# Fused attention, dense FFN and routed experts on one core: tiles moved back to multiples of 64 bytes, one block's routing put off, values one step later, two more staging tiles

## The chip, the cores and the metric

One core of one Trainium2 chip runs the whole program in one launch. The metric is the device time of one execution in microseconds (us); the kernel before was run three times, and the median is what the change is measured against. The profiled execution is a separate one, with its own time.

## The reference, cut to what matters

Three stages, one behind the other, in float32:

- attention over 8 batches, 8 heads, 576 tokens, with keys and values first averaged over groups of 8 tokens, so that each head has 72 keys;
- a dense feed-forward layer on the 4608 tokens of 512 numbers: `x @ w_in` (512 by 2048), ELU, `@ w_out` (2048 by 512);
- a routed layer: each token's row times `w_gate` gives 8 logits, the largest picks an expert, its softmax weight is the gate; the token goes through `relu(x @ w1[e]) @ w2[e]` of that expert (512 by 1024, 1024 by 512), and the result is scaled by the gate.

```
x = attention(q, pool8(k), pool8(v))
x = elu(x @ w_in) @ w_out
e = argmax(x @ w_gate);  out = gate_w * (relu(x @ w1[e]) @ w2[e])
```

## The kernel before, in words

**Precision.** Every large product is made of three float32r products: operands are split into a high part and a remainder (`xh`, `xl`; `gh`, `gl`; `wih`, `wil`; `woh`, `wol`; in the routed stage `zh`, `zl`, `m1h`, `m1l`, `hh`, `hl`, `m2h`, `m2l`), and high*high, high*low and low*high are added up in PSUM. TensorE is given a weight load and a matmul for each, 512 moving columns where a block has four tiles of 128 tokens, 384 where it has three.

**Blocks and steps.** The 36 token tiles are ten blocks: 0 to 3 of three tiles, 4 to 9 of four. A step is one of 16 slices of 128 hidden units of one block. `g1_mm` (L514) makes 12 matmuls into `h` (moving `xh`/`xl`, stationary `wih`/`wil`); `elu_a`, `elu_b`, `elu_c` (L527 to L546) run on ScalarE and VectorE and leave `gh` and `gl`; two steps later `g2` (L554) makes three matmuls a tile into `y` (stationary `gh`/`gl`, moving `woh`/`wol`). Blocks 0 and 1 take turns in quarters (steps 0 to 31, numbered by their place in `steps`); from step 32 each block has its 16 steps. Block 9's begin at step 144, and its end overlaps the routed stage.

**What rides along.** Beside the two products a step carries slices of other work, put into named slots by `at(n, slot, fn, ...)` (L727) and run by `step` (L893) in a fixed order: `pre`, the `h` matmuls, `pe_mid`, `dve_first`, `dve_pre`, ELU, `act_hi`, `act_mid`, the `y` matmuls, `pe_end`, `evac`, `dve_mid`, `elu_c`, `act_end`, `end`. Each engine takes its instructions strictly in that written order. For an attention tile `t` this is: `s_mm` (L409), scores, at `SCORE[t]`; `s_exp` and `s_norm` in that step and the next; `q_turn` (L455), a transpose on VectorE, one step on; `q_move` (L462) in two parts in the next two steps, whose 32-partition copies into `aT` are shared by ScalarE and VectorE; `pv_mm` (L485), the product with the values, at `VALUE[t]`; `pv_copy` (L496), which splits it into `xh` and `xl`. The last value tile must be through before a block's first step. `PLAN` (L757) gives the steps of a block's score products relative to the block before, and L769 the steps of the value products.

**Routing.** `route_at` (L862) spreads a block's logits over some ten steps. A logit of one tile and one expert is one VectorE instruction on 512 numbers (`r_logit` L619, into `junk`) against an expert's row that SyncE has loaded (`r_gate_load` L614, three buffers `wgb`). Then `r_top`, `r_weight` (which also makes SyncE store the rows with their gate to `ybuf`, L675), and, two steps after that, `r_count` (two small matmuls into `pos` on TensorE, L690) and `r_put` (L697), which lets GpSimd scatter the token numbers into `tab`. `pos` takes a PSUM bank from the ring of three that `sp` and `pv` use (`bank_a` L158; from step 62 a ring of two, `bank_z`). Block 0's logits (`route_at(0, 40, ...)`, L883) lie in steps 40 to 50, block 2's in 51 to 59, block 3's in 66 to 75, block 4's from step 82 on.

**The routed stage.** `mix(n)` (L1621) is a step of 24 + 24 matmuls (`mhD` L1358, `myD` L1395) on 512 tokens of one expert. `ahead(n)` (L1527) is the planner: by due times (`STEP`, reach 36 for loads, 25 for splits) it issues `m_load`, SyncE's loads of a quarter of an expert's two matrices into staging tiles, and `m_split`, the split on ScalarE and VectorE (L135, L136) into W slots. Staging tiles are numbered: 0 lies in the pool `p2a`, 2 to 4 in `p2b` (`free_s`, L1674); a D unit takes two, and gives them back at its split. By the planner's rules a load is written once a step, in the same step as the split whose tiles it takes over. `chores` (L1607) puts block 9's logits into steps 0 to 3 of this stage (eight a step), `r_top`, `r_weight`, `r_place`, `lists_rest` into steps 4 to 7.

**Where tiles lie.** On the left of each partition: `cpool`, then `wpool` (32 slots W of 4096 bytes, which hold `wih` to `wol` and later `m1h` to `m2l`), then `apool` and `spool`, whose place `p2a` takes in the routed stage. On the right, from the top down: `mrpool`, then `m1pool`, whose place `p2b` takes. Tiles are rounded up to 32 bytes. The starts in the program before, as the remainder by 512:

```
W slots 32 | hh, hl 32 | zh, zl 288      (routed stage: W, p2a)
gh, gl and xh, xl of blocks 0 3 5 7 9: 352   (m1pool)
xh, xl of blocks 1 2 4 6 8: 480              (apool)
```

All slices that matmuls take inside these tiles step by multiples of 512 bytes, so the remainder holds for each of them. All are 32 past a multiple of 64.

Of the kernel before, what the change touches and what calls it, by code (L numbers as in the profile page):

```python
# [10 lines left out]
F32 = mybir.dt.float32  # L11
# [8 lines left out]
P = 128  # L20
# [10 lines left out]
START = [sum(SIZES[:x]) for x in range(NBLK + 1)]  # L31
# [3 lines left out]
NF = DFF // P  # L35
NE = 8
KC = DM // P
ROW = DM + 1
# [64 lines left out]
def fused_kernel(ctx: ExitStack, tc: tile.TileContext, q, k, v, w_in, w_out, w_gate, w1, w2, cst, out):  # L103
# [3 lines left out]
    cpool = ctx.enter_context(tc.tile_pool(name="cpool", bufs=1))  # L107
# [12 lines left out]
    def const(at, n):  # L120
        return small[:, at - C_W:at - C_W + n]
# [4 lines left out]
    eidx, part = const(C_E, NE), const(C_J, 1)  # L126
# [14 lines left out]
    m1_ctx = ExitStack()  # L141
    at_ctx = ExitStack()
    mrpool = ctx.enter_context(tc.tile_pool(name="mrpool", bufs=1, side="right"))
    m1pool = m1_ctx.enter_context(tc.tile_pool(name="m1pool", bufs=1, side="right"))
    apool = at_ctx.enter_context(tc.tile_pool(name="apool", bufs=1))
    spool = at_ctx.enter_context(tc.tile_pool(name="spool", bufs=4))
# [26 lines left out]
    free_w, slot_w = list(range(W_SLOTS - 1)), {"sums": W_SLOTS - 1}  # L173

    def w_tile(shape, dtype, name):
        slot_w[name] = k = free_w.pop(0)
        return wpool.tile(shape, dtype, tag=f"W{k}", bufs=1, name=name)

    def w_free(*names):
        for name in names:  # L180
            free_w.append(slot_w.pop(name))
# [327 lines left out]
    ys, yrows, lgs, pes = {}, {}, {}, {}  # L509
# [64 lines left out]
    def y_rows(blk, plus=None):  # L574
        yr = mrpool.tile([P, TB, ROW], F32, tag="yr", name=f"yr{blk}")
        yrows[blk] = [yr[:, j] for j in range(TB)]
        if SIZES[blk] > TB:
            if blk < last - 1:
                yrows[blk].append(spool.tile([P, S], F32, tag="st", name=f"yx{blk}")[:, :ROW])
            else:  # L580
                yrows[blk].append(w_tile([P, ROW], F32, f"yx{blk}"))
        for j, r in enumerate(yrows[blk]):
            if plus:
                nc.vector.tensor_add(r[:, :DM], plus[j], ys[blk][j])
            elif j < 2:
                nc.scalar.copy(r[:, :DM], ys[blk][j])  # L586
            else:
                nc.vector.tensor_copy(r[:, :DM], ys[blk][j])
        return yr
# [68 lines left out]
    def r_weight(blk):  # L658
        lg = lgs.pop(blk)
        mx, mb, eq = tops.pop(blk)  # L660
        yr = yrows[blk]
        nb = SIZES[blk]
        pool = lpool["p"] if blk == NBLK - 1 else mrpool

        def small_tile(shape, tag, dtype=F32):
            return pool.tile(shape, dtype, tag=tag, name=f"{tag}{blk}")

        se = mrpool.tile([P, nb], F32, tag="rse", name=f"rse{blk}")
        nc.vector.tensor_reduce(se, lg, axis=AX.X, op=ALU.add)
        nc.vector.tensor_scalar_add(se, se, 1e-9)  # L670
        for j in range(nb):
            nc.vector.reciprocal(yr[j][:, DM:ROW], se[:, j:j + 1])
        for j in range(nb):
            r = P * (START[blk] + j)
            nc.sync.dma_start(ybuf[r:r + P, :], yr[j])  # L675
        if f"yx{blk}" in slot_w:
            w_free(f"yx{blk}")
        nc.vector.tensor_mul(eq, eq, wge.unsqueeze(1).to_broadcast([P, nb, NE]))
        nc.vector.tensor_reduce(mx, eq, axis=AX.X, op=ALU.max)
        oh = small_tile([P, nb, NE], "roh", BF16)  # L680
        nc.vector.tensor_tensor(oh, eq, mb, op=ALU.is_equal)
        for j in range(nb):
            nc.vector.tensor_add(acc[:, j + 1], acc[:, j], oh[:, j])
        routed[blk] = oh, [small_tile([P, nb, NE], "rpe"), small_tile([P, nb], "rpf"), small_tile([P, nb], "rpi", I32)]
# [38 lines left out]
    LAG = 2  # L723
    last = NBLK - 1
    events = {}

    def at(n, slot, fn, *args):  # L727
        events.setdefault((n, slot), []).append((fn, args))
# [12 lines left out]
    def turn_at(t, n):  # L741
        at(n + 1, "end", q_turn, t)
        for part in range(2):
            at(n + 2 + part, "act_end" if part and t == START[4] else "act_mid", q_move, t, part)

    def trans_at(t, n):
        at(n, "pe_end" if t in OUT else "pe_mid", t_mm, t)
# [6 lines left out]
    at(2 * NF - 2, "end", s_wide)  # L754
    first_of = {b: b * S // P for b in range(B)}
    SCORE = {6: (20, "pe_mid"), 7: (24, "pe_mid"), 8: (28, "pe_mid")}
    PLAN = {3: (-1, 4, 9), 4: (-2, 2, 6, 10), 5: (-3, 1, 4, 8)}  # L757
    TRANS = {6: 23, 7: 26, 8: 30}
    OUT = {
        6: ((28, "pe_end"), (29, "pre")),  # L760
        7: ((29, "pe_end"), (30, "pre")),
        8: ((31, "pe_mid"), (31, "act_mid")),
    }
    VALUE = {}
    for t in range(START[3], NT):
        blk, j = BLOCK[t]
        SCORE[t] = (NF * (blk - 1) + PLAN.get(blk, (-4, 0, 4, 8))[j], "pe_mid")
        if t > START[3]:
            VALUE[t - 1] = SCORE[t][0] + (t == START[5]) + 2 * (t > START[5])  # L769
    VALUE[NT - 1] = NF * (NBLK - 1) - 2  # L770
    for t in range(2 * TB, NT):
        if t >= START[3]:
            if t > T_TURN:
                at(VALUE[t - 1], "pe_mid", pv_mm, t - 1)
                at(VALUE[t - 1], "act_mid", pv_copy, t - 1)
            at(SCORE[t][0] - 6, "end", a_load, t)
# [7 lines left out]
    at(NF * 4 - 2, "end", early.update, {"two": True})  # L784
    at(VALUE[NT - 1], "pe_mid", pv_mm, NT - 1)
    at(VALUE[NT - 1], "act_mid", pv_copy, NT - 1)
    for b in range(2, B):
        n0 = SCORE[first_of[b]][0]
# [44 lines left out]
    for x, (w, c) in enumerate(chunks):  # L833
        n = 2 + x
# [24 lines left out]
    for x in range(8):  # L859
        at(QF + 1 + x // 2, "end", gate_copy, x)  # L860

    def route_at(blk, n0, per):  # L862
        at(n0 - 3, "end", r_gate_load, blk, 0)
        at(n0 - 2, "end", r_gate_load, blk, 1)
        at(n0 - 1, "end", r_gate_load, blk, 2)
        n = 0
        nb = SIZES[blk]
        for x in range(NE * nb):
            e, j = divmod(x, nb)
            at(n0 + n, ("dve_mid", "end", "end", "end")[x - sum(per[:n])], r_logit, blk, e, j)  # L870
            if j == nb - 1 and e + 3 < NE:
                at(n0 + n, "end", r_gate_load, blk, e + 3)
            if x + 1 == sum(per[:n + 1]):
                n += 1
        n += n0
        at(n, "dve_mid", r_top, blk)
        at(n + 1, "dve_mid", r_weight, blk)
        if blk < last - 1:
            at(n + 3, "pe_mid", r_count, blk)
            at(n + 3, "end", r_put, blk)  # L880

    route_at(1, 30, [2, 3, 3, 1, 1, 2, 3, 3, 3, 3])
    route_at(0, 40, [2] * 9 + [3, 3])  # L883
    route_at(2, 3 * NF + LAG + 1, [2, 2, 3, 3, 3, 3, 2, 3, 3])
    for blk in range(3, last):
        per = [4, 3, 3, 3, 3, 3, 4, 3, 3, 3] if SIZES[blk] > TB else [3, 2, 3, 2, 3, 2, 3, 2, 2, 2]
        route_at(blk, NF * (blk + 1) + LAG, per)

    def run(n, slot):
        for fn, args in events.pop((n, slot), ()):  # L890
            fn(*args)
# [131 lines left out]
    def new(shape, name, dtype=F32):  # L1023
        return lpool["p"].tile(shape, dtype, name=name)
# [6 lines left out]
    def counts(tag):  # L1031
        pc = bank_z([P, NE], f"cp{tag}")
        nc.tensor.matmul(pc, ones, acc[:, 0], start=True, stop=True)
        cnt = new([P, NE], f"cnt{tag}")
        nc.vector.tensor_copy(cnt, pc)
        return cnt
# [99 lines left out]
    def lists_first():  # L1136
        full = above(counts("w"), thrf[:, 1::2], "w")
        regs, oh, _ = make_list(full, basee, KD, "w", 2 * ST)
        used = cpool.tile([P, NE], F32, name="used")
        nc.vector.tensor_add(used, oh[:, 0], oh[:, 1])  # L1140
        for s in range(2, KD):
            nc.vector.tensor_add(used, used, oh[:, s])
        nc.vector.tensor_scalar_mul(used, used, 2.0)
        for s in range(KD):
            where["D", s] = (regs, s)
        lpool["used"] = used
# [26 lines left out]
    pools = []  # L1173
# [3 lines left out]
    free_s, slot_s = [0], {}  # L1177
# [314 lines left out]
    n0 = len(steps) - NF  # L1492
# [67 lines left out]
    for k in range(1, len(main)):  # L1560
        kind, prev = main[k][0], main[k - 1][0]
        for u in range(TILES[kind]):
            if kind == "T":
                n = 4 * k - 2
            elif prev == "T":
                n = 4 * k - TILES[kind] + u
            else:
                n = 4 * k - 1
            (trans_late if prev != "T" and u > 1 else trans_at).setdefault(n, []).append((main[k], u))
    moves, casts_first = {}, set()  # L1570
    for k in range(TURN_FROM, len(main)):
        it, far = main[k], main[k - 1][0] == "T"
        if it[0] != "T":
# [3 lines left out]
            n = 4 * k - 4 if far else 4 * k - 1  # L1577
# [20 lines left out]

    def logits(n):
        nb = SIZES[last]  # L1600
        for x in range(2 * nb * n, 2 * nb * (n + 1)):
            e, j = divmod(x, nb)
            r_logit(last, e, j)
            if j == nb - 1 and e + 3 < NE:
                r_gate_load(last, e + 3)

    chores = {n: [(logits, n)] for n in range(4)}  # L1607
    chores[4] = [(r_top, last)]
    chores[5] = [(r_weight, last)]
    chores[6] = [(r_place, last)]  # L1610
    chores[7] = [(lists_rest,)]
    chores[8] = [(make_lists, 0)]
    chores[11] = [(make_lists, 1)]

    def index(x, *fns):
# [55 lines left out]
        y_evac(last)  # L1671
    m1_ctx.close()
    pools.append(ctx.enter_context(tc.tile_pool(name="p2b", bufs=1, side="right", reuse_waits="tile")))
    free_s += [2, 3, 4]  # L1674
    with tc.manual_schedule(engines=ENGINES):
        ahead(0)
        for n in range(7):
# [94 lines left out]
```

## Time and profile before

| | us |
|---|---|
| median of 3 runs | 1375.26 (1372.09 to 1376.05) |
| profiled execution, its own time | 1370.78 |
| its span, first to last instruction | 1369.0 |
| TensorE busy in the span | 1341.8 (98%) |
| VectorE busy | 1016.8 (74%) |
| ScalarE busy | 796.6 (58%) |

TensorE is busy nearly throughout, but "busy" counts an instruction from its start to its modelled end: how fast matmuls follow each other has to be read from the chain of waits, which gives stretches of matmuls with start, length and count. In the listings below PE is TensorE, DVE VectorE, ACT ScalarE, POOL GpSimd, SP SyncE (SPq its queue).

### The profile page before, as it was taken

The numbers are of one execution on the slowest core, as the hardware profiler recorded it, in microseconds if no ns is written. First come the engines' busy times: TensorE is split into PE (matmuls) and PEld (weight loads), VectorE is DVE, ScalarE is ACT, GpSimd is POOL, SyncE is SP. The second block draws the span as 40 slices with busy tenths as digits, with TensorE's granted clock in tenths as the row PEclk, the third lists the DMA queues.
The fourth block names the chain that finished last, engine by engine and source line by source line (L and its number), as shares of the span: only waits on it lengthen the run. The fifth ranks groups of instructions, "written<-read, shape, count | busy, mean of one in ns | idle before, by whom it ended". The sixth has DMA issues, their size and how long they took to land.

```text
span 1369.0 us, 22633 instructions
## 1 busy us (share of the span) xinstructions
PE 1341.8 (98%) x7977; PEld 1097.4 (80%) x7978; DVE 1016.8 (74%) x2301; ACT 796.6 (58%) x1855; POOL 276.5 (20%) x249
## 2 busy tenths in 40 slices
PE   8999999989999999999999999999999999999998
PEld 5798888878777777777777777888777888878787
DVE  7899889878787797796886886875867756747362
ACT  6777866757766656666666654462355445536261
POOL 4665411011112111121100000111213130222010
PEclk9999999989999999999999999999999999999999
DMA  9367535666657347349216202746686557597580
GB/s 337 123 188 211 148 82 111 56 104 46 96 64 92 38 78 76 30 81 88 37 35 70 32 24 39 125 121 93 185 138 117 168 173 234 197 304 243 196 281 23
DMA packets 107203, 167.26 MB, mean 122 GB/s; under 512 B 15501, under 2 KB 53007, under 8 KB 107024
## 3 DMA queue, kind: packets, MB, share of 16 engines
q1 hardware_dynamic: 89224, 131.25, 42.1%
q0 software_dynamic: 17856, 34.46, 12.8%
q8 instruction: 65, 1.06, 0.4%
q14 instruction: 58, 0.48, 0.2%
HBM read 144.26 MB, written 23.98 MB: 123 GB/s over the span
## 4 chain that ended last, share of the span: by engine, by line
PE 84%; DVE 5%; issue 4%; DMA 3%; ACT 3%; SPq 1%; POOL 1%; POOLq 0%; another core or an unknown queue 0%; ACTq 0%; DVEq 0%
PE y L564 28%; PE h L520 28%; PE mhD L1358 11%; PE myD L1395 11%; PE pv L492 3%; PE sp L423 2%; DMA w2stD<-in_moe_w_dram 1%; DVE junk L626 1%; DMA oidxT<-tab 1%; PE vsum L358 1%; POOL out_dram L1418 1%; DMA natv<-in_v_dram 0%; DVE g L537 0%; PE uh L1439 0%; DVE aT L467 0%
## 5 line engine op out<-in xcount | busy, mean ns | idle before, releaser
L564 PE MATMUL y<-woh,gh 128*128 128x512 f32 x576 | 234.1, 406 | 0.1
L564 PE MATMUL y<-wol,gh 128*128 128x512 f32 x576 | 228.1, 396 | 0.0
L564 PE MATMUL y<-woh,gl 128*128 128x512 f32 x576 | 228.1, 396 | 0.0
L530 ACT ACTIVATE th<-h 128x512 f32<-128x512 f32 (+1 forms) x160 | 89.0, 556 | 189.9 <-PE h L520 189.4
L537 DVE SCALAR_TENSOR_TENSOR g<-g,th 128x512 f32<-128x512 f32 (+1 forms) x160 | 102.6, 641 | 105.7 <-ACT th L532 104.9
L520 PE MATMUL h<-xh,wih 128*128 128x512 f32 (+1 forms) x640 | 162.1, 375 | 1.4 <-ACT xh L506 1.4
L520 PE MATMUL h<-xl,wih 128*128 128x512 f32 (+1 forms) x640 | 160.3, 372 | 0.1
L520 PE MATMUL h<-xh,wil 128*128 128x512 f32 (+1 forms) x640 | 159.4, 371 | 0.0
L626 DVE SCALAR_TENSOR_TENSOR junk<-yr,wgb 128x512 bf16<-128x512 f32 x216 | 148.5, 688 | 6.1 <-ACT yr L586 2.5
L1372 ACT ACTIVATE hhD<-mhD 128x512 fp32r<-128x512 f32 x64 | 38.3, 599 | 173.7 <-PE myD L1395 166.7
L544 ACT CAST gh<-g 128x512 fp32r<-128x512 f32 (+1 forms) x160 | 92.9, 580 | 78.5 <-DVE g L538 62.8
L520 PEld LDWEIGHTS h<-xh,wih 128*128 128x128 f32 x640 | 117.8, 189 | 24.3 <-ACT xh L506 1.9
L520 PEld LDWEIGHTS h<-xl,wih 128*128 128x128 f32 x640 | 117.8, 189 | 17.7 <-DVE xl L507 0.4
L520 PEld LDWEIGHTS h<-xh,wil 128*128 128x128 f32 x640 | 117.7, 188 | 16.9
L564 PEld LDWEIGHTS y<-woh,gh 128*128 128x128 f32 x576 | 108.4, 188 | 27.8 <-issue 3.6
L564 PEld LDWEIGHTS y<-woh,gl 128*128 128x128 f32 x576 | 108.5, 188 | 26.0
L707 POOL DMA_INDIRECT tab<-toki,rpi x36 | 39.2, 1089 | 435.2 <-DMA tab<-toki,rpi 221.6
L564 PEld LDWEIGHTS y<-wol,gh 128*128 128x128 f32 x576 | 108.6, 189 | 21.4
L1373 DVE SCALAR_TENSOR_TENSOR hlD<-mhD,hhD 128x512 fp32r<-128x512 f32 x64 | 44.1, 690 | 106.7 <-ACT hhD L1372 106.5
L545 DVE TENSOR_TENSOR gl<-g,gh 128x512 fp32r<-128x512 f32 (+1 forms) x160 | 103.1, 644 | 24.6 <-ACT gh L544 19.2
L538 DVE TENSOR_TENSOR g<-g,h 128x512 f32<-128x512 f32 (+1 forms) x160 | 101.4, 634 | 5.5
L1395 PE MATMUL myD<-m2hD,hhD 128*128 128x512 f32 x256 | 100.2, 391 | 0.0
(250 smaller groups left out, 2545.3 us busy)
## 6 DMA issues: line engine op xcount, KB each, us to landing
wgb<-gate_rows SPq DMA_DIRECT2D x80, 256.0 KB
w1stD<-in_moe_w_dram SPq DMA_DIRECT2D x32, 512.0 KB
w2stD<-in_moe_w_dram SPq DMA_DIRECT2D x32, 512.0 KB
qT<-in_q_dram SPq DMA_DIRECT2D x36, 256.0 KB
raw<-in_moe_w_in_dram SPq DMA_DIRECT2D x16, 512.0 KB
raw<-in_moe_w_out_dram SPq DMA_DIRECT2D x15, 512.0 KB
ybuf<-yr SPq DMA_DIRECT2D x27, 256.5 KB
t1U<-in_moe_w_dram SPq DMA_DIRECT2D x12, 512.0 KB
```

The costliest lines, as they stand in the source:

```text
L492: nc.tensor.matmul(ps[D * o:D * (o + 1), pr, p0:p0 + n], vs[b][:, h], aT[:, h, p0:p0 + n], start=True, stop=True)
L520: mark["g1"] = nc.tensor.matmul(ps, wi[i][a][:, c, o:o + P], bb[blk][:, c, :], start=n == 0, stop=n == 3 * KC - 1).ins
L530: nc.scalar.activation(th, hps[blk, f], AF.Relu, scale=-1.0)
L537: nc.vector.scalar_tensor_tensor(g, g, 1.0, th, op0=ALU.add, op1=ALU.mult)
L538: nc.vector.tensor_max(g, g, hps.pop((blk, f)))
L544: nc.scalar.copy(gh, g)
L545: nc.vector.tensor_sub(gl, g, gh)
L564: nc.tensor.matmul(ys[blk][j], a[:, js], wo[i][bb][:, o, :], start=n == 0 and f in FIRST[blk], stop=n == 2 and f in LAST[blk],)
L626: nc.vector.scalar_tensor_tensor(junk, yrows[blk][j][:, :DM], 1.0, pes[blk, e], op0=ALU.mult, op1=ALU.mult, accum_out=lgs[blk][:, j, e:e + 1])
L1358: mark["g1"] = nc.tensor.matmul(ps[:, x], a[:, c, o * P:(o + 1) * P], y[:, c], start=k == 0, stop=k == len(terms) - 1).ins
L1373: nc.vector.scalar_tensor_tensor(hl, ps, 0.0, hh, op0=ALU.max, op1=ALU.subtract)
L1395: nc.tensor.matmul(yps[it][u], a[:, us], second[w][:, o], start=i == 0 and o == 0 and n == 0, stop=i == 3 and o == 1 and n == 2,)
```

## The change

Four things, in one diff:

1. Sizes and places of small tiles. `used` (32 bytes) goes from `cpool` to `p2a`; `mrpool` gets a first tile `align_g` of 352 bytes that nothing uses; the fourth tile's row of blocks 8 and 9 (`yx`) goes from a W slot into `p2a` as its first tile, 2528 bytes of which 2052 are used. The starts become, as the remainder by 512: W 0; `gh`, `gl` and `xh`, `xl` of blocks 0 3 5 7 9: 0; `hh`, `hl` 0; `zh`, `zl` 256; `xh`, `xl` of blocks 1 2 4 6 8: 448. All are multiples of 64.
2. Routing. Block 0's logits of experts 0 to 4 stay in steps 40 to 47; those of experts 5 to 7 go to steps 77 to 79, with `r_top`, `r_weight`, `r_count` and `r_put` at 80, 81 and 83 (before 51, 52 and 54). Block 2's logits start a step earlier and end a step later (50 to 60), mostly two a step.
3. Attention. The scores of tiles 12 and 15 come a step earlier (45 and 57), the values of tiles 13 and 14 a step later (55 and 59); the value of tile 12 stays at 50, that of 15 at 62. The second part of tile 12's `q_move` is no longer put off to the end of its step.
4. Routed stage. Staging tiles 5 and 6 are added; block 9's logits are spread over five steps instead of four, and the chores behind them move one step down.

```diff
     mrpool = ctx.enter_context(tc.tile_pool(name="mrpool", bufs=1, side="right"))
+    mrpool.tile([P, 88], F32, name="align_g")
...
-                yrows[blk].append(w_tile([P, ROW], F32, f"yx{blk}"))
+                yrows[blk].append(pools[0].tile([P, 632], F32, tag="yx", name=f"yx{blk}")[:, :ROW])
...
-        if f"yx{blk}" in slot_w:
-            w_free(f"yx{blk}")
...
-            at(n + 2 + part, "act_end" if part and t == START[4] else "act_mid", q_move, t, part)
+            at(n + 2 + part, "act_mid", q_move, t, part)
...
-    PLAN = {3: (-1, 4, 9), 4: (-2, 2, 6, 10), 5: (-3, 1, 4, 8)}
+    PLAN = {3: (-1, 4, 9), 4: (-3, 2, 6, 9), 5: (-3, 1, 4, 8)}
...
-    VALUE = {}
+    VALUE, LATER = {}, {12: 1, 14: 1, 15: 2, 16: 1}
...
-            VALUE[t - 1] = SCORE[t][0] + (t == START[5]) + 2 * (t > START[5])
+            VALUE[t - 1] = SCORE[t][0] + LATER.get(t, 2 * (t > START[5]))
...
-    def route_at(blk, n0, per):
+    def route_at(blk, n0, per, e0=0, e1=NE):
...
+        if e1 < NE:
+            return
...
-    route_at(0, 40, [2] * 9 + [3, 3])
-    route_at(2, 3 * NF + LAG + 1, [2, 2, 3, 3, 3, 3, 2, 3, 3])
+    route_at(0, 40, [2] * 7 + [1], 0, 5)
+    route_at(2, 3 * NF + LAG, [2, 2, 2, 2, 2, 2, 3, 2, 2, 2, 3])
...
+        if blk == 3:
+            route_at(0, 77, [3, 3, 3], 5, NE)
...
-        used = cpool.tile([P, NE], F32, name="used")
+        used = new([P, NE], "used")
...
-        for x in range(2 * nb * n, 2 * nb * (n + 1)):
+        for x in range(NE * nb * n // 5, NE * nb * (n + 1) // 5):
...
-    chores = {n: [(logits, n)] for n in range(4)}
-    chores[4] = [(r_top, last)]
+    chores = {n: [(logits, n)] for n in range(5)}
+    chores[5] = [(r_top, last)]
...
-    free_s += [2, 3, 4]
+    free_s += [2, 3, 4, 5, 6]
```

`r_weight`, `r_place`, `lists_rest` and `make_lists` 0 go from steps 5, 6, 7 and 8 to 6, 7, 8 and 9 in the same way; `make_lists` 1 stays at 11.

## Rows read from the trace of the kernel before

**Rows 1.** The page, head and part 1: busy time by engine.
```profile
span 1369.0 us, 22633 instructions
PE 1341.8 (98%) x7977; PEld 1097.4 (80%) x7978; DVE 1016.8 (74%) x2301; ACT 796.6 (58%) x1855; POOL 276.5 (20%) x249
```

**Rows 2.** Groups of PE by shape: busy us, mean ns, then idle before them.
```profile
L564 PE MATMUL y<-woh,gh 128*128 128x512 f32 x576 | 234.1, 406 | 0.1
L520 PE MATMUL h<-xh,wih 128*128 128x512 f32 x384 | 105.3, 396 | 0.0
L1395 PE MATMUL myD<-m2hD,hhD 128*128 128x512 f32 x256 | 100.2, 391 | 0.0
```

**Rows 3.** Chain of waits, 920 to 946 us: start us, us, what.
```profile
924.26 5.47 PE mhD L1358 x24
929.73 5.60 PE y L564 x24
...
940.79 5.21 PE myD L1395 x23
```

**Rows 4.** Chain of waits, dense stage: blocks 3, 6 (580 us) and 7 (644 us).
```profile
274.45 2.10 PE h L520 x12
...
583.63 2.79 PE h L520 x12
586.42 2.80 PE y L564 x12
...
644.67 2.76 PE h L520 x12
```

**Rows 5.** Windows, steps 46, 50, 54: length, busy of PE, PEld, DVE, ACT, POOL; PEclk.
```profile
247.96:254.02 6.06, 6.06 (x70) 5.16 (x69) 5.45 (x14) 4.14 (x14) 0.00 (x0) 1.00 1.13 26
...
266.58:274.28 7.70, 6.12 (x70) 5.19 (x69) 7.03 (x19) 6.24 (x20) 0.00 (x0) 1.00 0.69 63
...
286.83:301.70 14.87, 9.22 (x88) 7.79 (x87) 9.57 (x27) 5.88 (x19) 0.88 (x1) 0.66 0.96 126
```

**Rows 6.** Waits of PE: waiting line, releaser, us in total, times, longest.
```profile
PE pv L492 <- DVE aT L467: 5.7, 4, 1.7
PE pos L694 <- DVE xl L507: 3.9, 1, 3.9
PE mhD L1358 <- DVE hlD L1373: 3.0, 3, 2.3
...
PE zTD L1287 <- DVE gateD L1278: 1.2, 1, 1.2
```

**Rows 7.** Waits of all engines: the row of GpSimd's scatters into `tab`.
```profile
POOL tab L707 <- DMA tab<-toki,rpi: 221.6, 25, 15.0
```

**Rows 8.** A logit by its tile (min/median/max ns), and windows of steps 77 and 78.
```profile
L626 DVE SCALAR_TENSOR_TENSOR junk<-yr,wgb x216: 649/691/732, 179.2 to 979.4; 128x512 bf16<-128x512 f32 x108
...
424.35:429.94 5.59, 5.59 (x25) 4.50 (x24) 1.71 (x5) 3.21 (x10) 1.02 (x2) 1.00 0.34 48
429.94:436.76 6.82, 6.82 (x42) 5.28 (x40) 6.41 (x23) 4.70 (x13) 1.47 (x2) 1.00 0.98 142
```

**Rows 9.** Chain of waits, routed stage, 955 to 1070 us.
```profile
965.91 0.70 DVE junk L626 x2
...
1004.98 17.80 DMA w2stD<-in_moe_w_dram
...
1027.63 0.70 DVE hlD L1373
...
1028.37 7.35 PE mhD L1358 x24
```

**Rows 10.** Order of time on SP, 1001 to 1005 us: start, us, instruction.
```profile
1001.55 1.30 SPq L675 DMA_DIRECT2D ybuf<-yr  x3
...
1004.05 0.69 SPq L1308 DMA_DIRECT2D w1stD<-in_moe_w_dram  x1
```

More of the change, by code (lines that the diff above doesn't have):

```diff
@@ L860, in fused_kernel @@
         at(QF + 1 + x // 2, "end", gate_copy, x)
-    def route_at(blk, n0, per):
-        at(n0 - 3, "end", r_gate_load, blk, 0)
-        at(n0 - 2, "end", r_gate_load, blk, 1)
-        at(n0 - 1, "end", r_gate_load, blk, 2)
+    def route_at(blk, n0, per, e0=0, e1=NE):
+        for x in range(3):
+            at(n0 - 3 + x, "end", r_gate_load, blk, e0 + x)
         n = 0
         nb = SIZES[blk]
-        for x in range(NE * nb):
-            e, j = divmod(x, nb)
+        for x in range((e1 - e0) * nb):
+            e, j = e0 + x // nb, x % nb
             at(n0 + n, ("dve_mid", "end", "end", "end")[x - sum(per[:n])], r_logit, blk, e, j)
-            if j == nb - 1 and e + 3 < NE:
+            if j == nb - 1 and e + 3 < e1:
                 at(n0 + n, "end", r_gate_load, blk, e + 3)
@@ L1605, in logits @@
                 r_gate_load(last, e + 3)
-    chores = {n: [(logits, n)] for n in range(4)}
-    chores[4] = [(r_top, last)]
[L1609 to L1612, printed above, removed]
+    chores = {n: [(logits, n)] for n in range(5)}
+    chores[5] = [(r_top, last)]
+    chores[6] = [(r_weight, last)]
+    chores[7] = [(r_place, last)]
+    chores[8] = [(lists_rest,)]
+    chores[9] = [(make_lists, 0)]
     chores[11] = [(make_lists, 1)]
```

## The prediction

> **What bounds the kernel now.** The page comes first: TensorE is busy in 1341.8 of 1369.0 us [rows 1]. So a gain has to come from three places: how fast matmuls follow each other, the few stops, and stretches at the lower clock. An engine that works beside TensorE counts only where TensorE stops for it.
>
> Pace first. The groups by shape give counts, not pace, since their means include the overlap: 406, 396 and 391 ns for shapes that all have 512 columns [rows 2]. The chain gives the pace. In the routed stage 23 `myD` took 5.21 us, 226.5 ns each; in the dense stage 12 `y` took 2.80 us, 233.3 ns each [rows 3, 4]. It isn't the stage that differs: between two groups of the routed stage lie the last 24 `y`, with the same kind of moving operand from W slots and with neighbours of their own size, and they still took 5.60 us, 233.3 ns [rows 3]. What those `y` have and `myD` hasn't is the stationary operand: `gh`, `gl` in the right pool instead of `hh`, `hl` in the left one. By the list of starts both are 32 past a multiple of 64, so "not a multiple of 64" alone can't be the cause. But `hh` has W's remainder by 512 and `zh` differs from it by 256, while `gh` differs by 320. I read it so: a pair of operands whose starts differ by a multiple of 256 runs at 226.5 ns, and other distances can cost up to 6.8 ns more.
>
> Then the stops. TensorE waited four times for `aT` before values, 5.7 us, and once 3.9 us for a bank for `pos` [rows 6]. The windows show where: step 46, with scores and values, took 6.06 us and no idle time; step 50 7.70; step 54, with scores, values and `pos`, 14.87, at a mean granted clock of 0.66, part of it at the lower of the two levels, after the idle time [rows 5]. In the routed stage there is a stop of 2.3 us and one of 1.2 [rows 6].
>
> **The change part by part.**
>
> *Sizes of tiles.* W, `gh` and `hh` all come to remainder 0, `zh` to 256. All 1728 `y` (3 x 576 [rows 2]) should then go at the pace of `myD`: 1728 x 6.8 ns = 11.8 us. Bounds: nothing, and the same again. Blocks 5, 7 and 9 have `xh`, `xl` in the right pool too: 576 matmuls, in groups of 2.76 or 2.79 us for 12 [rows 4], mean 231 ns, so 576 x 4.7 ns = 2.7 us. Blocks 4, 6 and 8 keep a distance of 448, as before: 0, at best 576 x 6 = 3.5 us. Groups of 384 columns took 2.10 us, 175 ns [rows 4]; 128 columns less than 226.5 ns at 2.4 GHz would be 173 ns, so they hardly pay the extra now: 0. The pairs of the routed stage keep their distance: 0. Together 14.5 us. The new place of `yx` costs nothing: its writers and readers stay.
>
> The Trainium skill ("TensorE: Matmul & The Clock Gate", section "Step-by-step: what each phase is for") says that weight load and moving operand have independent read ports, so that loading the next weights takes no bandwidth from the running matmul. By that rule place would not matter and this term would be 0; the trace disagrees, 5.60 us for 24 against 5.21 for 23 [rows 3].
>
> *Values and scores.* The four late `aT` come at steps 50, 54, 58 and 62, each late by at most 1.7 us [rows 6]. Each of the four gets one step more between its scores and its values, 4.2 us (2.10 for `h` [rows 4] and nine `y` of 233 ns), and tile 12's last copies come before its step's end. VectorE also loses load there: two logits a step instead of two or three, and no `r_top`, `r_weight` of block 0. So all 5.7 us go. The work of the steps stays, in other steps: 0. *Routing of block 0.* `pos` leaves step 54. There TensorE waited because `pos` needs the bank of `pv`, whose evacuation by VectorE stood behind the softmax maxima and ELU; at step 83 neither scores nor values stand beside it, so 3.9 us go. With the idle time the lower clock goes: step 54 was busy 9.22 us for work that takes 6.06 in step 46 [rows 5], 3.2 us. Sum of both parts 12.8 us.
>
> What the move puts elsewhere: nine logits at 77 to 79, 0.69 us each and a short read of the sum, which I allow 0.08, so 6.9 us on VectorE. Steps 77 and 78 have 1.71 + 6.41 = 8.1 us busy in 12.4 [rows 8]; six logits make that 12.7, so VectorE runs late by a fraction of a microsecond into 79. The products there lie two steps ahead of their use, and values two steps behind the last copies: 0. SyncE's three row loads and three stores move from near 52 to 74 to 81; it has no other work that can't wait a step there. GpSimd's three scatters go to 83, in front of batch 6's key links; at 221.6 / 25 = 8.9 us each [rows 7] they hold that queue for 27 us, and the links start at 84 for scores at 104, twenty steps of 5.6 to 6.8 us [rows 8]: 0.
>
> *Routed stage.* Spreading the logits takes eight a step down to 6 or 7: 1.6 x 0.77 = 1.2 us less VectorE work a step. The stop of 1.2 us stands right behind logits [rows 6, 9], so it goes. The stop of 2.3 us hangs on a load: `w2st` took 17.8 us from 1004.98 on, its split and `lists_rest` came late on VectorE, `hlD` behind them at 1027.63, and the next 24 `mhD` took 7.35 us instead of 5.47 [rows 3, 9], 1.9 us of lower clock. With a third pair of tiles, a load no longer waits for its own step's split. And the load that was late is now written before block 9's `r_weight`, not behind its stores (at 1001.55 before the load at 1004.05 [rows 10]). It can start up to a step sooner, 24 `mhD` and 24 `myD`, near 10.7 us [rows 3]. Bounds: nothing, 4.2 us. I take 4.2, since the load's own wait is what the rows show last; together 5.4 us.
>
> **Sum.** 14.5 + 12.8 + 5.4 = 32.7 us. The profiled execution took 1370.78, so 1338.1 for one like it. It lies 4.5 us under the median of the runs shown; against that median, 1375.26 - 32.7 = 1342.6.
>
> **The rivals.**
>
> *The stop in the routed stage comes back a step later.* `r_weight` moves by a step, and the next step's load then stands behind its stores, just as before. For it: the order on SyncE is the same one step on. Against: the load before it has landed by then, and no second one competes. 4.2 us less gain: 1346.8.
>
> *Place is not the cause.* Something else about `gh` makes `y` slow, or the starts that matter are others. For it: the list can't tell remainders by 256 from by 512, and one pool differs from the other in more than its start. Against: 24 `y` among `mhD` [rows 3]. Then 18.2 us remain: 1357.1.
>
> *Multiples of 64 count themselves.* All operands are off by 32 now, so even 226.5 ns may hold a cost. For it: 512 columns at 2.4 GHz are 213.3 ns. Against: no row shows an aligned pair, and nothing ties the rest to starts. One more step of 6.8 ns on 1728 + 1152 + 1536 matmuls of 512 columns (three products each of the shapes in [rows 2]) is 30.0 us: 1312.6. The Trainium skill (the same page, "Back-to-back issue gap") gives N/2.4 + 2.5, 215.8 ns at 512 columns. By that there are 10.7 ns to gain a matmul; the trace has no such matmul of this type.
>
> *Slower: aligned starts collide.* If two reads from the same remainder 0 get in each other's way, the same 4416 matmuls lose a step of 6.8 ns, 30.0 us, against 18.2 gained elsewhere: 1387.1. It decides from 18.2 / 0.0068, some 2700 matmuls, on. Against it: `hh` and W share a remainder now, at the fastest pace there is [rows 3].
>
> *VectorE falls behind at 77 to 83.* 12.7 us of work in 12.4, then `r_weight` and `r_put` beside block 4's rows. If TensorE stops there as in step 54 and the clock falls, 14.87 - 6.06 = 8.8 us [rows 5]: 1351.4. Against: no row of this stage shows a wait.
>
> **How the numbers follow.** Forecast 0.54; stop comes back 0.14; place not the cause 0.10; multiples of 64 0.12; VectorE late 0.05; collision 0.05. Predicted 1342.6. The range takes in all but the third and the collision, 0.83: at the top 1357.1 and a little, 1358; at the bottom the forecast with 3.5 us for blocks 4, 6 and 8 and the runs' own spread of 4 us, 1335. The likeliest case alone is 1337 to 1347. A run can tell 0.3%, some 4 us. All cases but the collision are faster by more: faster 0.94, same 0.01, slower 0.05.
>
> **What the changed profile would show.** Right: groups of 12 `y` of 2.72 us, of 12 `h` 2.72 in blocks 5, 7, 9 and 2.79 in 4, 6, 8; `myD` unchanged; no wait of `pv` or `pos`; PEclk full around 290 us; no 7.35 us group. Wrong: `y` still 2.80 us; `myD` other than 226.5 ns; idle time of TensorE at steps 77 to 83; a late `w2st` one step on.

## The result, and the profile after

The changed kernel takes 1358.43 us (median of 4 runs, 1357.23 to 1359.86), the kernel before 1373.67 beside it (1368.58 to 1376.05): a ratio of 0.9894, 95% interval 0.9863 to 0.9926. It is faster by some 15 us, 1.1%, where 32.7 were forecast; the predicted 1342.6 is too low, and the time lies just above the range. The profiled execution took 1358.63 us.

The head of the page, against [rows 1]; PE's busy time fell by 5.8 us and the span by 12.2:

```profile
span 1356.8 us, 22640 instructions
PE 1336.0 (98%) x7977; PEld 1098.5 (81%) x7978; DVE 1013.2 (75%) x2301; ACT 794.9 (59%) x1855; POOL 276.2 (20%) x249
```

The waits of PE and DVE, against [rows 6] (waiting line, releaser, us in total, times, longest):

```profile
PE h L521 <- DVE g L539: 2.9, 1, 2.9
PE mhD L1360 <- DVE hlD L1375: 2.8, 2, 1.5
PE sp L424 <- DVE rpe L700: 2.3, 2, 1.4
...
PE zTD L1289 <- DVE gateD L1280: 0.4, 1, 0.4
...
DVE rpi L704 <- DMA tab<-toki,rpi: 8.0, 1, 8.0
```

The late `aT` (5.7 us) and the bank for `pos` (3.9) are gone, and so is the stop of 2.3 us in the routed stage. Three rows are new: `h` waits for `g`, `sp` for `rpe`, and VectorE 8.0 us for a scatter. The stops of `mhD` are other ones, of 1.5 and 1.3 us.

The chain of waits from step 80 on (start us, us, what) follows the new stop back:

```profile
435.18 8.63 DMA tab<-toki,rpi
...
444.26 9.63 DMA tab<-toki,rpi
...
454.15 14.27 DMA tab<-toki,rpi
...
468.50 0.17 DVE rpi L704
...
471.37 0.70 DVE g L539
...
472.11 5.49 PE h L521 x12
```

`r_put` of block 3 (step 79) writes three columns of places into `rpi`, and GpSimd's three scatters hold it one behind another until 468.42, GpSimd waiting for each to land, as in [rows 7]. `rpi` has one buffer. Before the change the next block to write it came 16 steps later; now `r_put` of block 0 comes at step 83 and stands on VectorE from 460.4 to 468.5. Behind it in VectorE's order are block 4's logits, softmax maxima and the ELU that gives `g` and reads `h` from its PSUM bank. Two such banks take turns, so the 12 `h` of step 86 wait 2.9 us for that ELU, and then they take 5.49 us. The windows of steps 83 and 84, of step 85, and of step 86 (length, busy of PE, PEld, DVE, ACT, POOL, then PEclk, DMA share, GB/s) show the clock with it, 1.00 before the stop and 0.69 behind it, part of that step at the lower of the two levels:

```profile
449.99:463.60 13.61, 12.24 (x83) 9.66 (x82) 10.14 (x28) 6.74 (x13) 1.00 (x1) 1.00 1.10 90
463.60:472.11 8.51, 5.60 (x25) 4.32 (x23) 3.54 (x10) 1.32 (x8) 0.97 (x1) 0.95 0.01 3
472.11:481.74 9.63, 9.63 (x40) 7.30 (x41) 9.16 (x23) 7.64 (x20) 1.31 (x1) 0.69 0.43 33
```

The chain in the dense stage, blocks 6 and 7, against [rows 4]:

```profile
568.91 2.74 PE y L565 x12
571.65 2.80 PE h L521 x12
...
641.77 2.72 PE y L565 x12
644.50 2.72 PE h L521 x12
```

That is the forecast pace: `y` 2.72 or 2.74 for 2.80, `h` 2.72 for 2.76 in block 7, still 2.80 in block 6.

Where the time went, by the starts of the steps' first `h` in the two traces (the second row is the kernel before with the new sizes alone, the third the new order alone, both from the experiments below; some 25 us ahead of step 0 are left out):

| steps | 0-15 | 16-31 | 32-65 | 66-79 | 80-87 | 88-143 | 144-158 | the rest |
|---|---|---|---|---|---|---|---|---|
| before | 83.46 | 76.41 | 171.41 | 85.88 | 48.74 | 341.67 | 85.47 | 450.62 |
| sizes alone | 82.66 | 76.34 | 169.46 | 85.32 | 47.86 | 337.68 | 83.75 | 452.77 |
| order alone | 84.21 | 76.42 | 159.41 | 85.88 | 51.29 | 341.67 | 85.47 | 449.29 |
| after | 84.09 | 76.34 | 159.12 | 85.32 | 56.99 | 337.68 | 83.75 | 448.16 |

The first column differs mostly by how long the lower clock near 31 us lasts (3.4 or 6.8 us in executions of kernels that are alike there); no edit is behind that. Steps 32 to 65 gave 12.3 us, steps 80 to 87 took 8.3 back, the other dense steps gave 6.3, the routed stage 2.5.

### The profile page after: what moved, and what is told of

It reads as the page before. It is cut to its first block, busy times and chain, and to the rows that moved or that the text cites. A ratio compares the mean times of both kernels' runs of the same rounds, so it can differ in the third digit from the quotient of the medians.

```text
span 1356.8 us, 22640 instructions
## 1 busy us (share of the span) xinstructions
PE 1336.0 (98%) x7977; PEld 1098.5 (81%) x7978; DVE 1013.2 (75%) x2301; ACT 794.9 (59%) x1855; POOL 276.2 (20%) x249
## 3 DMA queue, kind: packets, MB, share of 16 engines
q0 software_dynamic: 17856, 34.46, 12.8%
## 4 chain that ended last, share of the span: by engine, by line
PE 77%; DMA 10%; issue 8%; DVE 2%; ACT 1%; POOL 1%; SPq 1%; POOLq 0%; DVEq 0%; ACTq 0%
PE h L521 24%; PE y L565 24%; PE mhD L1360 11%; PE myD L1397 11%; DMA v<-in_v_dram 3%; DMA tab<-toki,rpi 3%; PE pv L493 2%; DMA kT<-in_k_dram 2%; PE sp L424 1%; DMA oidxT<-tab 1%; DVE junk L627 1%; PE vsum L359 1%; DMA natv<-in_v_dram 0%; DMA w2stS<-in_moe_w_dram 0%; PE uy L1466 0%
## 5 line engine op out<-in xcount | busy, mean ns | idle before, releaser
L565 PE MATMUL y<-wol,gh 128*128 128x512 f32 x576 | 225.3, 391 | 0.0
L565 PE MATMUL y<-woh,gl 128*128 128x512 f32 x576 | 225.1, 391 | 0.0
L521 PEld LDWEIGHTS h<-xl,wih 128*128 128x128 f32 x640 | 119.1, 189 | 16.9
L546 DVE TENSOR_TENSOR gl<-g,gh 128x512 fp32r<-128x512 f32 (+1 forms) x160 | 102.2, 639 | 19.9 <-ACT gh L545 14.8
```

Of the source, the lines that this page charges most:

```text
L521: mark["g1"] = nc.tensor.matmul(ps, wi[i][a][:, c, o:o + P], bb[blk][:, c, :], start=n == 0, stop=n == 3 * KC - 1).ins
L546: nc.vector.tensor_sub(gl, g, gh)
L565: nc.tensor.matmul(ys[blk][j], a[:, js], wo[i][bb][:, o, :], start=n == 0 and f in FIRST[blk], stop=n == 2 and f in LAST[blk],)
```

## The experiments

Each of these kernels is timed against the kernel before on the same chip, and its median is set beside the 1358.43 of the changed kernel.

**1. `rpi` of its own.** `rpi` is the suspected cause, VectorE's load the rival.

```diff
-    mrpool.tile([P, 88], F32, name="align_g")
+    mrpool.tile([P, 80], F32, name="align_g")
...
-        ... small_tile([P, nb], "rpi", I32)]
+        ... small_tile([P, nb], "rpi" if blk else "rpi0", I32)]
```

> The changed kernel, with block 0's `rpi` in a tile of its own (and 8 floats less of alignment, so that `gh`, `gl`, `xh`, `xl` start where they did). Steps 80 to 87 took 56.99 us in the changed kernel and 48.74 before, 8.25 more, around a wait of VectorE of 8.03 us for the scatters that read block 3's `rpi`. Theory A (the single `rpi` buffer is what stops the chip there): that wait is gone, TensorE has no stop above 0.5 us in these steps, they take 48 to 49 us, and the kernel 8 to 9 us less than the changed one, near 1350. Theory B (VectorE has too much to do there: 43.9 us busy against 39.1 before): the wait goes but the stops stay in another place, steps 80 to 87 still take over 54 us, and the kernel is within 3 us of the changed one.

Measured 1352.99 us (1351.06 to 1353.7), ratio to before 0.9865, interval 0.9827 to 0.9902; 5.4 us less than the changed kernel, with no overlap of the runs. VectorE's wait is gone and steps 80 to 87 take 51.11 us, 5.9 less. So theory A is right, but not for the whole: 3.2 us remain over the 47.86 of the sizes alone. What remains is in this chain, around step 84:

```profile
459.10 0.70 DVE junk L627 x2
459.80 0.60 DVE gl L546
460.40 0.10 DVE rpe L700
...
460.55 0.72 PE sp L424 x30
```

`sp` waits for the bank of `pos`, which `rpe` has to read, and `rpe` stands behind logits: two waits, 2.5 us here, which are theory B's part.

**2. The sizes alone.** The kernel before with the first part of the change (`align_g`, `used` in `p2a`, `yx` in its own tile).

```diff
+    mrpool.tile([P, 88], F32, name="align_g")
...
-        used = cpool.tile([P, NE], F32, name="used")
+        used = new([P, NE], "used")
...
-                yrows[blk].append(w_tile([P, ROW], F32, f"yx{blk}"))
+                yrows[blk].append(pools[0].tile([P, 632], F32, tag="yx", name=f"yx{blk}")[:, :ROW])
...
```

> The kernel before with the new sizes of tiles alone (alignment, `used` among the routed tiles, `yx` in a tile of its own); order of the work as before. By the step of the prediction: 14.5 us less than before, `y` 2.72 us for 12 in all blocks of 512 columns, `h` 2.72 in blocks 5, 7 and 9. By the changed kernel's own trace (groups of 384 columns 0.02 to 0.03 us slower for 12 `h`, faster by as much for 9 `y`; a longer lower clock at the start): 9 to 12 us less, near 1363. If the sizes had nothing to do with the pace, the time of before. The stops at steps 50 to 62 and the one at `pos` of block 0 stay as they were.

Measured 1361.68 us beside 1371.57, ratio 0.9931, interval 0.9896 to 0.9965: 9.9 us less (5 to 14). The profiled span fell by 7.7. The table shows where: 7.2 us from step 66 to 158, 0.07 in steps 16 to 31, though those have 144 `y` (the `h` beside them lost about what these gained; see below). The old stops stay (5.5 us for `aT`, 3.2 for `pos`), and the one in the routed stage is longer than in [rows 6]: `w2st` is issued as far behind the first `mhD` as before (80.8 us for 80.9), but its split starts 19.9 us after that (994.92 to 1014.86) and not 17.8. Why this load took longer, one trace doesn't tell.

```profile
PE mhD L1357 <- DVE hlD L1372: 4.4, 1, 4.4
```

**3. The order alone.** The changed kernel without the first part.

```diff
-    mrpool.tile([P, 88], F32, name="align_g")
...
-        used = new([P, NE], "used")
+        used = cpool.tile([P, NE], F32, name="used")
...
-                yrows[blk].append(pools[0].tile([P, 632], F32, tag="yx", name=f"yx{blk}")[:, :ROW])
+                yrows[blk].append(w_tile([P, ROW], F32, f"yx{blk}"))
...
```

> The changed kernel with the sizes of tiles of the kernel before: the order of the work and the staging tiles are changed, the starts are not. By the prediction's steps 18.2 us less than before, near 1353. By the trace of the changed kernel: 12.9 us less in steps 46 to 65, 8 us given back in steps 80 to 87, 2 to 4 less in the routed stage, together 5 to 8 less than before, 1364 to 1367. The wait for `rpi` came out at 8.0 us with a stop of TensorE of 2.9 us in the changed kernel and at 5.6 to 5.8 us with one of 0.3 to 0.5 us where only starts differ; if here the wait is nearer 5.6, the kernel is 5 us faster than that, near 1360.

Measured 1360.12 us beside 1369.07, ratio 0.994, interval 0.9921 to 0.9958: 9 us less, not 18.2. Steps 32 to 65 take 12.0 us less (12.8 were forecast); 2.6 come back in steps 80 to 87, and the routed stage gives 1.3. The wait for the scatters is there, but shorter, and no `h` waits for `g`:

```profile
DVE rpi L705 <- DMA tab<-toki,rpi: 4.7, 1, 4.7
```

So the shared `rpi` has a threshold: 4.7 us of waiting cost TensorE nothing, 8.0 us cost it 2.9 us of idle time and 6.8 us at the lower clock. Steps 80 to 87 take 5.7 us more in the changed kernel than here, which is more than what is missing where sizes and order, good for 9.9 and 9 us alone, gave 15 together.

**4. The left pool moved by 64 bytes.** If the distance of starts sets the pace, blocks 4, 6 and 8 can have it too.

```diff
     apool = at_ctx.enter_context(tc.tile_pool(name="apool", bufs=1))
+    apool.tile([P, 16], F32, name="align_x")
```

> The changed kernel with an unused tile of 64 bytes at the start of the left pool, so that `xh` and `xl` of blocks 4, 6 and 8 start at remainder 0 by 512 instead of 448, which is a multiple of 64 as well. Theory D (it is the distance of the two operands' starts by 256 that sets the pace, not the multiple of 64): 12 `h` of these blocks take 2.72 us instead of 2.80, 576 x 6.6 ns = 3.8 us, and the kernel is 4 to 5 us faster than the changed one, near 1354. Theory M (each start has to be a multiple of 64, no more): nothing changes, 1358. Theory P (it is the pool or the block, not the start): `h` stays at 2.80 us.

Measured 1349.20 us (1348.11 to 1350.39), ratio 0.9837, interval 0.98 to 0.9874; 9.2 us less than the changed kernel. The chain of block 6 and of step 83 on:

```profile
451.74 13.62 DMA tab<-toki,rpi
...
465.43 0.17 DVE rpi L705
...
469.04 3.06 PE h L522 x12
...
569.07 2.94 PE y L566 x12
572.01 2.72 PE h L522 x12
574.73 2.72 PE y L566 x12
```

`h` of block 6 goes at 2.72 us: theory D. Steps 66 to 158 without 80 to 87 take 4.0 us less (506.75 to 502.71). Another 4.9 us come from steps 80 to 87: the last scatter landed 3 us sooner there, VectorE waited 5.7 us, TensorE 0.5 us for `g`, and the clock held. In three runs TensorE's idle time is the wait less some 5.2 us: 0.3 of 5.6 (run 5), 0.5 of 5.7 here, 2.9 of 8.0 in the changed kernel; of these only the last was followed by the lower clock.

**5. The right pool 64 bytes off.** All starts are multiples of 64 here, too.

```diff
-    mrpool.tile([P, 88], F32, name="align_g")
+    mrpool.tile([P, 72], F32, name="align_g")
```

> The changed kernel with 64 bytes less of alignment: `gh`, `gl` and block 5's, 7's and 9's `xh`, `xl` start at remainder 64 by 512, still a multiple of 64, and 64 away from the W slots. Theory D (distance by 256): 12 `y` take 2.80 us again in every block of 512 columns and 12 `h` of blocks 5, 7 and 9 2.76 to 2.80, and the kernel is 12 to 16 us slower than the changed one, near 1372. Theory M (multiples of 64): 2.72 us as in the changed kernel, and its time, 1358.

Measured 1359.23 us in one execution. The pace is that of the kernel before, as theory D has it (block 6, then block 7):

```profile
574.24 2.79 PE h L521 x12
577.03 2.80 PE y L565 x12
...
647.65 2.76 PE h L521 x12
650.41 2.80 PE y L565 x12
```

The time missed the expectation by 13 us: steps 66 to 158 without 80 to 87 took 512.84 us, only 6.1 more than after, and steps 80 to 87 took 51.94, 5.1 less, with a wait for `rpi` of 5.6 us. Alignment to 64 bytes by itself is worth nothing; a slower pace happened to take the stop away.

**6. Both edits.** Own `rpi` and the left pool.

> The changed kernel with both edits that were tried one by one: block 0's `rpi` in its own tile, and the left pool moved by 64 bytes. Theory A with a threshold (VectorE has about 5 us in hand at step 84, so that the wait of 5.7 us with the moved left pool costs next to nothing): 0 to 1.5 us less than with the left pool alone, near 1348.5. Rival (the two gains add, 5.4 and 9.2 us): near 1343.8. In either case no wait of VectorE for the scatters at steps 80 to 87, and the waits of `sp` for `rpe`, 2.5 us in two, stay.

Measured 1349.10 us (1347.37 to 1350.11), ratio 0.986, interval 0.9839 to 0.9882: the time with the left pool alone, with steps 80 to 87 at 51.19 us for 52.07. The threshold holds, the rival is out. The own buffer is still worth having, since the wait's length hangs on when a scatter lands.

**7. Block 0's logits more slowly** (on run 6).

```diff
-            route_at(0, 77, [3, 3, 3], 5, NE)
+            route_at(0, 77, [1, 2, 2, 2, 2], 5, NE)
```

> As the run before, with block 0's nine logits over five steps from 77 on (1, 2, 2, 2, 2 in place of 3, 3, 3), so that its places are asked for at step 85 and not 83. Theory C (VectorE, full from 418 to 437 us with three logits a step, brings block 3's places and so the bank for `sp` late): the waits of `sp` for `rpe` at steps 80 and 84 go, 2 to 3 us less than the run before. Rival (VectorE's work in steps 77 to 87 is the same, so the wait only comes at another step): within 0.7 us of it, with a wait of about 1 us at step 86 or 88.

Measured 1346.31 us (1345.57 to 1347.06), 2.8 less than run 6. Steps 80 to 87 take 48.94 us where run 6 had 51.19, and no `sp` waits for `rpe` any more; the only wait for a bank there is this row:

```profile
PE pos L694 <- ACT s_wide L441: 0.5, 1, 0.5
```

So VectorE did fall behind at three logits a step; it cost some 2.3 us in these steps.

**8. The routed stage's logits unevenly** (on run 6).

```diff
-        for x in range(NE * nb * n // 5, NE * nb * (n + 1) // 5):
+        cut = [0, 8, 16, 22, 28, 32]
+        for x in range(cut[n] * nb // 4, cut[n + 1] * nb // 4):
```

> The changed kernel with its own tile for block 0's `rpi` and the left pool moved, and the 32 logits of block 9 over the first five steps of the routed stage as 8, 8, 6, 6, 4 in place of 6, 6, 7, 6, 7. Theory E (`hlD` is late at the sixth step because seven logits of the last portion stand ahead of it on VectorE): the stop of 1.54 us there goes, 1.5 us less than with the two edits alone; the next stop, 1.26 us behind `r_weight`, stays. Rival (the weights' splits and the zT copies on VectorE set it): the stop stays above 1 us.

Measured 1346.19 us (1345.05 to 1348.23), 2.9 less than run 6 (1.5 were expected); the two ranges overlap, but the traces agree: the routed stage takes 445.47 us for 448.01. In the changed kernel the chain runs through the last portion of logits into `hlD`, and again through block 9's `r_weight` at 1006:

```profile
981.74 0.71 DVE junk L627 x2
...
983.18 0.61 DVE hlD L1375
...
983.84 5.74 PE mhD L1360 x24
...
1006.48 0.69 DVE hlD L1375
```

Here the first stop is gone, with that of 0.4 us at the zT copies; the second is left, as theory E said:

```profile
PE mhD L1361 <- DVE hlD L1376: 1.3, 1, 1.3
```

**9. The routed stage's logits as before,** with the third pair of staging tiles (on run 7): eight a step over four steps, and the chores behind them a step earlier.

> The kernel with `rpi` of its own, the left pool moved and block 0's logits over five steps, and in the routed stage block 9's logits over four steps and all that follows a step earlier, as before the change; the third pair of staging tiles stays. If the pair alone took the late load away: no stop of over 2 us near 1010, no lower clock there, and the stops of 1.54 and 1.26 us become one near 1.2 us at the zT copies and one of 0.5 to 1.5 us behind the weights; within 2 us of 1346. If the order of loads and stores did it: the stop of 2 to 4.5 us with the lower clock is back, 4 to 6 us more, near 1351.

Measured 1344.72 us in one execution, 1.6 less than run 7; the routed stage takes 446.88 us where run 7 had 448.22. There are two stops, 1.1 us at the zT copies and 1.2 us here, and no lower clock:

```profile
982.45 16.57 DMA w2stD<-in_moe_w_dram
...
1003.84 0.69 DVE hlD L1376
...
1004.58 5.75 PE mhD L1361 x24
```

So spreading the logits bought nothing with the third pair in place. But the pair alone didn't do what it was credited with: `w2st` is issued 80.8 us after the first `mhD` (901.65), as before the change (1004.98, first `mhD` at 924.09: 80.9), and the same `hlD` hangs on it. It landed after 16.57 us and not 17.80 [rows 9], which one execution can't put down to an edit. In the changed kernel the same load, the sixth `w2st` behind the first `mhD` (914.21), goes out after 64.0 us, ahead of block 9's stores, on the timeline of SP:

```profile
978.19 0.38 SPq L1320 DMA_DIRECT2D w2stD<-in_moe_w_dram  x1
...
1002.81 1.31 SPq L676 DMA_DIRECT2D ybuf<-yr  x3
```

So the later chores are needed to bring that load forward; whether they do it without the pair wasn't run.

**10. 128 bytes apart** (on run 6).

```diff
-    mrpool.tile([P, 80], F32, name="align_g")
+    mrpool.tile([P, 48], F32, name="align_g")
```

> The kernel with `rpi` of its own and the left pool moved, and the right pool's `gh`, `gl`, `xh`, `xl` 128 bytes from the W slots by 512 in place of 0; blocks 4, 6 and 8 have `xh`, `xl` at distance 0. By the prediction's reading (a distance that is a multiple of 256): 12 `y` take 2.80 us, 12 `h` of blocks 5, 7 and 9 2.76 or more, 12 `h` of blocks 4, 6 and 8 2.72; about 14 us more than 1349. If a multiple of 128 is enough: 2.72 us everywhere, and its time.

Measured 1359.01 us in one execution, 10 more than run 6 (some 14 were expected). Block 6, then block 7:

```profile
575.10 2.77 PE h L522 x12
577.87 2.80 PE y L566 x12
...
648.04 2.79 PE h L522 x12
650.83 2.80 PE y L566 x12
```

A distance of 128 is as slow as one of 64. `h` of block 6, whose own distance is 0, stands between slow `y` and comes out at 2.75 to 2.77 us: a group's time also hangs on its neighbours.

**11. The W slots 32 bytes off** (on run 1).

```diff
-        used = new([P, NE], "used")
+        used = cpool.tile([P, NE], F32, name="used")
```

> The kernel with `rpi` of its own, and `used` back in front of the W slots, so that these start at 32 by 512, while `gh`, `gl` and the right pool's `xh`, `xl` start at 0 (distance 32), and `hh`, `hl` keep the distance 0 to the W slots that hold `m2`. By the prediction's reading: 12 `y` 2.80 us, 12 `h` 2.76 to 2.80, 24 `myD` 5.44 as ever, about 12 us more than with `rpi` alone, 1365. If only the start of the moving or the stationary operand counts by itself, `myD` becomes slower too or `y` stays at 2.72 us.

Measured 1371.19 us in one execution. The expectation had one start wrong: `hh`, `hl` and `zh`, `zl` lie at 0 and 256 in this kernel, since `used` leaves their pool as it enters the one in front of it, so they lie 32 and 224 from the W slots. So the run tests whether the fast part can be made slow. Start, length and operands of two groups of 4 `mhD`, 20 matmuls apart, on the timeline of PE, first of the changed kernel:

```profile
935.97 1.07 PE L1360 MATMUL mhD<-zhD,m1hD 128*128 128x512 f32 x4
...
940.51 1.07 PE L1360 MATMUL mhD<-zhD,m1lD 128*128 128x512 f32 x4
```

Then of this one:

```profile
940.03 1.10 PE L1360 MATMUL mhD<-zhD,m1hD 128*128 128x512 f32 x4
...
944.70 1.10 PE L1360 MATMUL mhD<-zhD,m1lD 128*128 128x512 f32 x4
```

4.54 us for 20 there, 227 ns each; 4.67 here, 233.5. `y` and `h` are slow in all blocks of 512 columns, as expected. The routed stage, from step 159 on, takes 457.45 us for 447.67 in run 1: 1536 `mhD` and `myD` by 6.5 ns make 10.0, and 9.8 were measured. Before the change W and `hh` lay at 32 both, and after it at 0 both, at one pace (226.7 ns); it is the distance that counts, not the multiple.

**12. All four edits,** runs 1, 4, 7 and 8 in one kernel.

> All four edits on the changed kernel: block 0's `rpi` in its own tile, the left pool moved by 64 bytes, block 0's logits over five steps, block 9's logits as 8, 8, 6, 6, 4. If the two last ones add (2.8 and 2.9 us, in stages that don't touch): 1349.1 - 2.8 - 2.9 = 1343.4. Rival (a stop that is gone in one stage lets a load or a scatter collide in the next): no better than the better one of the two, 1346.

Measured 1343.45 us (1342.68 to 1345.21, 5 runs), ratio to before 0.982, interval 0.9796 to 0.9845. The two gains add (48.89 us for steps 80 to 87, 445.38 for the routed stage), and the median is 2.7 us under that of either.

## Why the prediction was right or wrong

**Right: the cause of the pace.** "... a pair of operands whose starts differ by a multiple of 256 runs at 226.5 ns": in blocks of 512 columns distances (by 512) of 0 and 256 do, 32, 64, 128, 224, 320 and 448 don't (runs 4, 5, 10 and 11, and [rows 3, 4]). *Place is not the cause* and *multiples of 64 count themselves* are out by the same runs: blocks 4, 6 and 8 were multiples of 64 and slow, and `myD` kept 226.7 ns from 32 and 32 to 0 and 0. The 3.5 us that the prediction allowed "at best" for blocks 4, 6 and 8 were real, 4.0 us, and took one more tile of 64 bytes.

The sentence on weight load and moving operand from the Trainium skill ("TensorE: Matmul & The Clock Gate", "Step-by-step: what each phase is for") would, as the prediction reads it, make their starts a matter of indifference; run 11 takes 6.5 ns a matmul more with nothing changed but their distance, so here that doesn't come out. Why the distance counts, no run tells.

**Wrong in size: 14.5 us for the sizes.** Run 2 gave 9.9 (5 to 14), its trace 7.7 of span. The failing step is "All 1728 `y` ... should then go at the pace of `myD`". By the starts in the traces of before and of run 2, in blocks of 512 columns the 600 `y` right behind `h` gained 5.9 ns each, but the 552 behind scores, values and other matmuls only 3.1. In blocks of 384 columns next to nothing came of it: in steps 16 to 45, where 270 of their 576 `y` lie, these gained 1.1 us of 1.8 forecast, and the 360 `h` beside them lost 0.7; 0.4 us are left (139.17 to 138.80). So the 0 for groups of 384 columns failed too: an `h` of 384 columns became some 2 ns slower.

Step 39 (block 2) shows it, in the changed kernel, where `xh` lies 448 from the W slots, and in run 4, which brings `xh` to 0 and leaves `gh`, `gl` and the W slots alone. First `y` of nine and next `h`, on the timeline of PE, changed kernel first:

```profile
219.14 0.39 PE L565 MATMUL y<-woh,gh 128*128 128x512 f32 x1
...
221.18 0.87 PE L521 MATMUL h<-xh,wih 128*128 128x384 f32 x4
```
```profile
219.38 0.39 PE L566 MATMUL y<-woh,gh 128*128 128x512 f32 x1
...
221.46 0.87 PE L522 MATMUL h<-xh,wih 128*128 128x384 f32 x4
```

Nine `y` in 2.04 us, 227 ns each, there, and in 2.08, 231 ns, here, with the same tiles at the same distance. So the pace of `y` also hangs on the matmuls ahead of it; why, no run tells.

**Right: values and scores, routing of block 0.** 12.8 us were forecast; steps 32 to 65 took 12.0 less with the order alone, and the five waits named and the lower clock near 290 us went.

**Wrong: "GpSimd's three scatters go to 83 ... they hold that queue for 27 us ...: 0".** The step that failed. The prediction followed the queue of the moved scatters forward and asked who stands behind them. It didn't ask what those of block 3, issued at 79, still hold when block 0's `r_put` comes four steps later: 33 us of scatters, with one buffer, against some 25 us until its next write. Own `rpi` is worth 5.4 us (run 1).

The prediction's 8.9 us a scatter was too low as well: at that, the wait would have been some 2 us and cost nothing (run 3). The third scatter took 14.27 us, 12.66 in run 3 and 13.62 in run 4, all with block 0's rows stored at step 81, and 8.27 in run 2, without these stores there. That the stores make it slow is likely, but no run changes them alone.

The price of *VectorE falls behind at 77 to 83*, 8.8 us, is near the 8.3 that steps 80 to 87 took, but that is luck: its mechanism is the smaller part, the 2.8 us of run 7, and it had 0.05 of the chance. "VectorE runs late by a fraction of a microsecond into 79" left out that ScalarE's and VectorE's `aT` copies and block 3's `r_put` share those steps, and that the ring of two banks lets `sp` wait for `pos`.

**Half right: routed stage, 5.4 us.** Against before it gave 2.5; against run 2, whose load took 19.9 us (452.77), 4.6. The long stop and its lower clock went, and the load did start sooner, by 16.9 us from the first `mhD`; but the third pair alone doesn't bring that (run 9). The rival of a stop a step later had its condition, the next load stands behind the stores (1005.69), but no stop of TensorE hangs on it. That the stop of 1.2 us "goes" failed: it fell to 0.4, and new stops of 1.5 and 1.3 us came, one behind a last portion of seven logits, one behind `r_weight` and the split of the `zm` copies. Fewer logits a step on the average is no fewer in the last step.

## What to carry to other kernels

When a step is moved, list not only the queues it joins but each single-buffered tile it writes, and who still reads it: here the next write of an index tile waited until an indirect DMA had landed, 14 us after its issue. A wait on an engine off the path cost nothing up to its slack (some 5.2 us here), then idle time, and with 2.9 us of that the clock; so measure parts in combination, since a gain in one place (here the pace) can push a wait in another over the edge. For float32r products of 512 columns put the pool of the stationary and of the moving operand at the same remainder by 256; a tile of a few dozen bytes does it.

## What the runs showed of the hardware that was not expected

- Among matmuls of 512 columns a 128x512 float32r matmul follows the one before in 226.7 ns with starts 0 or 256 apart by 512, and in some 230 to 233.5 ns at every other distance that was run (32, 64, 128, 224, 320, 448). 1536 matmuls of the routed stage lost 9.8 us to 32 bytes.
- The fast pace also hangs on what comes before: `y` of 512 columns behind `h` of 384 ran at 227 ns from the first on where that `h` lay 448 from its weights, and at 231 ns where it lay 0 from them.
- Three scatters of 128 numbers each kept the next write of their index tile waiting until the last had landed, 33 us after the first began (435.18 to 468.42).
- Stops of 1.5 us left the granted clock at 1.00; with the one of 2.9 us the lower level came for 6.8 us, and the step behind it had 0.69.
